# Linear attention with softmax features and a gated MLP: softmax without extrema, transposed queries, a lagging down projection

## The chip, the cores and the metric

One core of a Trainium2 chip runs the kernel. The metric is the device time of one execution in microseconds; the time before is 304.11 us, the median of three runs (303.58 to 304.22). The engines are PE (TensorE matmul, with its weight loads as PEld), DVE (VectorE), ACT (ScalarE), POOL (GpSimd) and SP, which issues most DMAs. Each works through its own instructions in order and waits on semaphores for the others.

## The reference

The input is 2048 tokens of width D = 512 in bf16; there are H = 32 heads of 16.

```python
mod = silu(c) @ w_mod                       # sa, ca, ga, sb, cb, gb
h = layernorm(x) * (1 + ca) + sa
q, k, v = split(h @ wqkv)                   # 32 heads of 16
pq, pk = q @ w_phi, k @ w_phi               # per head, 16 x 16
phi = concat(softmax(p), softmax(-p))       # 32 features, for q and for k
kv, z = phi_k^T v, sum_s phi_k              # per head
o = (phi_q kv) / (phi_q z + 1e-6)
x = x + ga * (o @ wo)
h = layernorm(x) * (1 + cb) + sb
x = x + gb * ((sigmoid(h @ w_gate) * (h @ w_up)) @ w_down)   # F = 1376
```

## The kernel before

Tokens are worked in 16 tiles of 128. The setup loads the weights through SP's queue, folds w_phi into the K part of wqkv (`fold_a_piece` transposes, `fold_b_piece` multiplies with the block diagonal `bd`, lines 226 to 248), computes the modulation columns `modc`, and normalizes the first tokens: `ln_stats` on DVE, `ln_small` and most `xn` on POOL, four transposes a column block on PE (`tp_h`), and the scaling into `h1T` on ACT or DVE.

The K loop (lines 476 to 522) runs over 20 items, the 16 K tiles and the first 4 Q tiles. An item is a software pipeline of stages: project into a PSUM bank (`p_bank`), take the largest and the smallest of each 16 on DVE (`s_maxmin`), subtract the largest from the bank by a matmul with the identity and exponentiate, undo it and subtract the smallest by two more matmuls and exponentiate the negative, sum and take reciprocals on DVE (`s`, `r`), multiply on POOL (`phi`). K tiles then add `phi` times `vaug` into `kvacc`; Q tiles are transposed by a DMA into `phiqT`.

When all K tiles are in, `kv_blockdiag` cuts out the head blocks, and the first four tiles pass through the attention output, the residual `x1` and the second LayerNorm one after the other (lines 515 to 529).

The GLU stretch goes over four chunks of 512 tokens. For each of 11 pieces of F it computes `g_ps` and `u_ps`, `tg` = tanh on ACT, `hm` on DVE, and at once four matmuls of the down projection into `y_ps`, which accumulate in four banks. Between the pieces, hooks work on the next chunk's queries, attention and LayerNorm. In the setup and the K loop the order on each engine is that of the program; in the GLU stretch a scheduler may interleave.

```python
            act.activation(tg[:fsz, :], g_ps[:fsz, :], ACT.Tanh, scale=0.5)
            dve.scalar_tensor_tensor(hm[:fsz, :], tg[:fsz, :], 1.0, u_ps[:fsz, :], op0=ALU.add, op1=ALU.mult)
            for tl in range(4):
                pe.matmul(y_ps[tl][:], lhsT=hm[:fsz, tl * P:(tl + 1) * P], rhs=wd_sb[:fsz, ft, :],
                          start=(ft == 0), stop=(ft == FT - 1))
```

In the profile nearly every instruction has line 47, that of the helper which records the order, so rows are told apart by the names of their tiles.

Of the kernel before, what the change touches and what calls it, by code (L numbers as in the profile page):

```python
# [9 lines left out]
BF16 = mybir.dt.bfloat16  # L10
ACT = mybir.ActivationFunctionType
ALU = mybir.AluOpType
AX = mybir.AxisListType

_SCHED = mybir.DependencyInfo(mybir.DependencyClass.NoSync, mybir.DependencyReason.SCHED_ONLY)


class _Ordered:

    def __init__(self, tc, eng):  # L20
        self._tc = tc
        self._eng = eng
        self._last = None
        self._fence = None
        self.strict = False

    def _note(self, r):
        ins = getattr(r, "ins", None)
        if ins is None:
            return r  # L30
        if self.strict and self._last is not None:
            self._tc.add_manual_dep(ins, self._last.name, _SCHED, reason="program order")
        elif self._fence is not None:
            self._tc.add_manual_dep(ins, self._fence.name, _SCHED, reason="phase fence")
        self._last = ins
        return r

    def fence(self):
        self._fence = self._last

    def __getattr__(self, name):
        f = getattr(self._eng, name)
        if not callable(f):
            return f

# [7 lines left out]
def kernel(  # L53
# [12 lines left out]
    CW = 68  # L66

    pe = _Ordered(tc, nc.tensor)
    act = _Ordered(tc, nc.scalar)
    dve = _Ordered(tc, nc.vector)  # L70
    pool = _Ordered(tc, nc.gpsimd)
    sp = _Ordered(tc, nc.sync)
    engines = (pe, act, dve, pool, sp)

    def set_strict(flag):
        for e in engines:
            if e.strict and not flag:
                e.fence()
            e.strict = flag

    consts = ctx.enter_context(tc.tile_pool(name="consts", bufs=1))
    psA_cm = tc.tile_pool(name="psA", bufs=1, space=bass.MemoryType.PSUM)
# [18 lines left out]
    ga_bc = consts.tile([P, D], FP32, name="ga_bc")
    gb_bc = consts.tile([P, D], FP32, name="gb_bc")
    mhalf = consts.tile([P, NT], FP32, name="mhalf")
    h1T = consts.tile([P, KT, S], BF16, name="h1T")
    vaug_all = consts.tile([P, NT, H, DH + 1], BF16, name="vaug_all")
    mask = consts.tile([P, 4, DH + 1], FP32, name="mask")
    kvbd_n = consts.tile([P, NG, 4 * DH], BF16, name="kvbd_n")
    kvbd_d = consts.tile([P, NG, 4], BF16, name="kvbd_d")
    stats = consts.tile([P, NT, 6], FP32, name="stats")
# [24 lines left out]
    sp.dma_start(x_sb[:, 0:4, :], x_v[:, 0:4, :])
    sp.dma_start(wqk_sb[:, :, D:2 * D], wqkv_v[:, :, D:2 * D])
# [13 lines left out]
    nc.gpsimd.memset(mhalf[:], -0.5)  # L149
    make_identity(nc, ident[:])  # L150
    bmask = setup.tile([P, P], BF16, name="bmask")
    make_block_diagonal(nc, bmask[:], DH)

    def ln_stats(src_ap, st, mvt, t):
        dve.bn_stats(st[:, t, :], src_ap)
        dve.bn_aggr(mvt[:, t, :], st[:, t, :])

    def ln_small(sl, mvt, vepst, rstdt, nmeant, nmrt=None):
        pool.tensor_scalar(vepst[:, sl], mvt[:, sl, 1], 1e-5, None, op0=ALU.add)
        pool.tensor_tensor(rstdt[:, sl], vepst[:, sl], mhalf[:, sl], op=ALU.pow)  # L160
        pool.tensor_scalar(nmeant[:, sl], mvt[:, sl, 0], -1.0, None, op0=ALU.mult)
        if nmrt is not None:
            pool.tensor_tensor(nmrt[:, sl], nmeant[:, sl], rstdt[:, sl], op=ALU.mult)

    def ln_xn(src_ap, t, rstdt, nmeant, nmrt, on_act):
        xn = lnp.tile([P, D], BF16, name="xn", tag="xn")
        if on_act:
            act.activation(xn[:], src_ap, ACT.Identity, scale=rstdt[:, t:t + 1], bias=nmrt[:, t:t + 1])
        else:
            pool.tensor_scalar(xn[:], src_ap, nmeant[:, t:t + 1], rstdt[:, t:t + 1], op0=ALU.add, op1=ALU.mult)  # L170
        return xn

    xn_box = {}

    def ln1_xn(t, on_act=False):
# [12 lines left out]
    def ln1_quarter(g, j, tag="tp"):
        ln_quarter([xn_box[4 * g + tl] for tl in range(4)], h1T[:, j, g * 512:(g + 1) * 512], j, 0, tag)

    ones11 = setup.tile([1, 1], BF16, name="ones11")
    nc.gpsimd.memset(ones11[:], 1.0)
    c_ps = ps_tile("c_ps", "tp", [P, 2 * KT])
# [15 lines left out]

# [434 lines left out]
```

## Time and profile before

| | |
|---|---|
| median of the runs | 304.11 us |
| profiled execution, span | 304.9 us |
| PE busy | 243.3 us (80%), 1524 matmuls seen |
| DVE busy | 193.2 us (63%) |
| ACT busy | 108.1 us (35%) |
| POOL busy | 116.0 us (38%) |
| mean granted clock of TensorE | 0.931 |

The busy shares are averages over stages that differ, so the rows below are cut by stage: setup to 17.5 us, K loop to 93.5, first attention tiles to 126 (the first `g_ps` starts at 125.9), GLU to 298.6. A granted clock of 1.00 is 2.4 GHz, 0.50 is 1.2 GHz. Matmul durations overlap, since the engine is pipelined; their pace is read from the starts.

### The profile page before, as it was taken

Reading aid. Unit: us, or ns where it says so; the run is one execution under the profiler, and the core shown is the slowest. Engines: PE = TensorE matmul, PEld = TensorE weight load, DVE = VectorE, ACT = ScalarE, POOL = GpSimd, SP = SyncE. Lnnn points to the kernel's source line nnn. Section 1 sums busy time; section 2 is a strip of 40 time slices with the busy share of each in tenths; the row PEclk is TensorE's granted clock in tenths of the full one; section 3 lists DMA queues with packets and bytes.
Section 4 is the critical chain, followed back from the end, with each engine's and each line's share of the span. In section 5 each row is a group of like instructions: output and inputs, shape, how many; then the busy total and the mean of one; then the engine's idle time right before and its main releaser. Section 6 shows DMA issues by size and latency. Waiting matters only on the chain. (4 is left out here: it accounts for less than half of the span.)

```text
span 304.9 us, 4096 instructions
## 1 busy us (share of the span) xinstructions
PE 243.3 (80%) x1524; PEld 115.6 (38%) x1552; DVE 193.2 (63%) x334; ACT 108.1 (35%) x185; POOL 116.0 (38%) x126
## 2 busy tenths in 40 slices
PE   0566988889774574599997899988799989499991
PEld 0533444444331342244443444443344443243330
DVE  3288899677989552167886288677287778052223
ACT  2454776765334033324311433301433311422110
POOL 2847379652556543974502222501313311400000
PEclk9995999999869567599999999999999999999996
DMA  6999400000001410001450021450021340020002
GB/s 186 384 399 400 153 2 1 1 2 0 2 0 34 85 21 0 0 0 35 71 105 0 0 69 37 70 105 1 0 69 38 69 91 14 0 69 0 2 0 69
DMA packets 31989, 19.71 MB, mean 65 GB/s; under 512 B 23921, under 2 KB 29410, under 8 KB 31970
## 3 DMA queue, kind: packets, MB, share of 16 engines
q1 hardware_dynamic: 31938, 19.44, 23.0%
q8 instruction: 12, 0.20, 0.3%
q0 software_dynamic: 32, 0.02, 0.2%
q14 instruction: 7, 0.06, 0.1%
HBM read 11.58 MB, written 2.10 MB: 45 GB/s over the span
## 5 line engine op out<-in xcount | busy, mean ns | idle before, releaser
L47 POOL TENSOR_TENSOR phi<-e,r 128x1024 bf16<-128x1024 bf16 x32 | 61.6, 1928 | 80.5 <-DVE r L47 65.2
L47 ACT ACTIVATE tg<-g_ps 128x512 bf16<-128x512 f32 (+1 forms) x44 | 26.2, 596 | 85.1 <-PE g_ps L47 76.5
L47 ACT ACTIVATE e<-p_bank 128x512 bf16<-128x512 f32 x64 | 38.3, 598 | 45.5 <-PE p_bank L47 43.1
L47 DVE SCALAR_TENSOR_TENSOR hm<-tg,u_ps 128x512 bf16<-128x512 bf16 (+1 forms) x44 | 30.0, 682 | 38.2 <-PE u_ps L47 28.4
L47 PE MATMUL g_ps<-h2T,wg_sb 128*128 128x512 bf16 (+1 forms) x170 | 49.2, 384 | 4.2 <-ACT tg L47 2.2
L47 PE MATMUL y_ps<-wd_sb,hm 128*128 128x512 bf16 (+1 forms) x170 | 46.3, 381 | 1.1 <-DVE hm L47 0.8
L47 PE MATMUL u_ps<-h2T,wu_sb 128*128 128x512 bf16 (+1 forms) x171 | 46.4, 385 | 0.5
L47 DVE TENSOR_REDUCE s<-e 128x64 f32<-128x1024 bf16 x32 | 38.6, 1207 | 6.5 <-ACT e L47 6.5
L47 PE MATMUL p_bank<-wqk_f,h1T 128*128 128x512 bf16 x125 | 35.3, 394 | 1.5 <-ACT h2T L47 1.3
L47 DVE TENSOR_REDUCE nmx<-p_bank 128x32 bf16<-128x512 f32 x32 | 21.5, 672 | 20.3 <-PE p_bank L47 20.3
L47 PEld LDWEIGHTS <-h1T 128*128 128x128 bf16 x192 | 19.2, 101 | 26.1 <-issue 6.5
L47 POOL TENSOR_SCALAR veps<-mv 128x4 f32<-128x4 f32 (+1 forms) x11 | 2.5, 228 | 62.7 <-DVE mv L47 57.2
L47 PEld LDWEIGHTS <-wg_sb 128*128 128x128 bf16 (+1 forms) x176 | 17.3, 101 | 22.3 <-issue 5.2
L47 PEld LDWEIGHTS <-hm 128*128 128x128 bf16 (+1 forms) x176 | 14.3, 97 | 27.8 <-DVE hm L47 16.9
L47 PEld LDWEIGHTS <-wu_sb 128*128 128x128 bf16 (+1 forms) x176 | 17.5, 101 | 19.1 <-issue 1.1
L47 DVE TENSOR_REDUCE nmn<-p_bank 128x32 bf16<-128x512 f32 x32 | 21.5, 672 | 0.0
L47 PE MATMUL tp_h<-ident,xn 128*128 128x128 bf16 x112 | 12.1, 239 | 11.7 <-POOL xn L47 10.7
L47 PE MATMUL a_ps<-wo_sb,oT 128*128 128x512 bf16 x62 | 18.6, 423 | 3.2 <-ACT oT L47 2.9
L47 PE MATMUL p_bank<-nmx,nident 128*128 128x512 bf16 x32 | 12.5, 391 | 8.6 <-ACT e L47 8.5
L47 DVE RECIPROCAL r<-s 128x64 f32<-128x64 f32 x32 | 17.6, 550 | 2.2
L47 PEld LDWEIGHTS <-xn 128*128 128x128 bf16 x128 | 9.5, 109 | 23.4 <-POOL xn L47 14.8
L47 PE MATMUL v_ps<-wv_sb,h1T 128*128 128x512 bf16 x58 | 17.0, 397 | 0.7 <-ACT h1T L47 0.4
(83 smaller groups left out, 286.8 us busy)
## 6 DMA issues: line engine op xcount, KB each, us to landing
x_sb<-in_A_x_dram SPq DMA_DIRECT2D x4, 512.0 KB, 10.0
wmod_sb<-in_w_mod_dram SPq DMA_DIRECT2D x1, 2048.0 KB, 14.8
out_dram<-ot SPq DMA_DIRECT2D x16, 128.0 KB, 1.8
wg_sb<-in_B_w_gate_dram SPq DMA_DIRECT2D x1, 1376.0 KB, 17.8
wu_sb<-in_B_w_up_dram SPq DMA_DIRECT2D x1, 1376.0 KB, 18.1
wd_sb<-in_B_w_down_dram SPq DMA_DIRECT2D x1, 1280.0 KB, 16.7
wqk_sb<-in_A_wqkv_dram SPq DMA_DIRECT2D x2, 512.0 KB, 8.2
wmod_sb<-in_w_mod_dram SPq DMA_DIRECT2D x1, 1024.0 KB, 8.3
```

The lines of the kernel that those rows point to most:

```text
L47: return self._note(f(*a, **k))
```

## The change

The kernel is written anew with every engine's order by hand:

- Softmaxes take no extrema: exp(p) and exp(-p) come straight from the projection. A bound on |p| is computed on the chip from the folded weights and the modulation; a flag says whether it is too large, and after the last output a branch runs a general path with extrema and writes all outputs again.
- K tiles keep sum, reciprocal and `phi`; LayerNorm's `xn` moves from POOL to DVE. `kvacc` holds 8 heads by 136 columns instead of 4 by 68.
- Queries are projected transposed (`q_blk`: weights as the stationary side, 512 tokens as the moving one), exponentiated into `eT` with no sums and no transposes. Sums and denominators come out of small matmuls (`sm`), four small DVE ops form the factors `cc`, and each of the two halves of the numerator is multiplied by its factor (`u`); the Q weights for the fold are transposed by their load.
- The chunks are of 2, 2, 4, 4, 4 tiles, and the down projection of a chunk is issued during the next one, tile by tile in two banks; the last chunk's follows at the end. The attention and LayerNorm steps of later tiles are put between the pieces by a list of due times.

On DVE, in the K loop, a tile before (`nmx`, `nmn` extrema, `s` and `r` sum and reciprocal):

```order
L47 BN_STATS stats<-x_sb 128x6
L47 BN_AGGR mv<-stats 128x2
L47 TENSOR_REDUCE nmx<-p_bank 128x32
L47 TENSOR_REDUCE nmn<-p_bank 128x32
L47 TENSOR_REDUCE s<-e 128x64
L47 RECIPROCAL r<-s 128x64
```

The same place now, tile 3 and the beginning of tile 4 (`ksum` and `kr` are sum and reciprocal):

```order
L130 BN_STATS st_77<-x_sb 128x6
L131 BN_AGGR mv_78<-st_77 128x2
L235 TENSOR_REDUCE ksum<-e 128x64
L237 RECIPROCAL kr<-ksum 128x64
L141 TENSOR_SCALAR xn<-x_sb,mv_78,rs_80 128x512 x4
```

The extrema are gone, and four `xn` stand behind the sum of a group's last tile.

On ACT, in the K loop, before:

```order
L47 CAST vaug_all_81<-v_ps_406 128x32x16
L47 ACTIVATE h1T_80<-tp_h_426,modc_76 128x512
L47 ACTIVATE e_434<-p_bank_392 128x32x16 x2
L47 CAST vaug_all_81<-v_ps_441 128x32x16
L47 ACTIVATE h1T_80<-tp_h_469,modc_76 128x512
L47 COPY wT0_477<-tp_w_478 128x512
```

and now (`e` and `h1T` as before; the bank `tp_h` of a tile is the next token group's):

```order
L226 CAST vaug1_108<-v_ps_329 128x32x16
L152 ACTIVATE h1T_70<-tp_h_340,modc_75 128x512
L231 ACTIVATE e_346<-k_ps_335 128x512 x2
L226 CAST vaug2_109<-v_ps_357 128x32x16
L152 ACTIVATE h1T_70<-tp_h_368,modc_75 128x512
```

`e` of a tile stands behind the `h1T` written in that tile, as it did before; what feeds that `h1T` is now the `xn` above, and POOL's `phi` and `rstd` ahead of it.

On PE, in a chunk of four tiles of the GLU stretch, before (`y_ps0` to `y_ps3` are the four tiles of the same chunk):

```order
L47 LDWEIGHTS wg_sb_71
L47 MATMUL g_ps_2882<-h2T_2765,wg_sb_71 128x512
L47 LDWEIGHTS hm_2876
L47 MATMUL y_ps0_2824<-wd_sb_73,hm_2876 128x512
L47 LDWEIGHTS hm_2876
L47 MATMUL y_ps1_2825<-wd_sb_73,hm_2876 128x512
L47 LDWEIGHTS hm_2876
L47 MATMUL y_ps2_2826<-wd_sb_73,hm_2876 128x512
L47 LDWEIGHTS hm_2876
L47 MATMUL y_ps3_2827<-wd_sb_73,hm_2876 128x512
L47 LDWEIGHTS wu_sb_72
L47 MATMUL u_ps_2883<-h2T_2765,wu_sb_72 128x512
```

and now (chunk 2; `hm_1605` belongs to chunk 1):

```order
L602 LDWEIGHTS wu_sb_68
L602 MATMUL u_ps_2023<-h2T_1675,wu_sb_68 128x512
L570 LDWEIGHTS hm_1605
L570 MATMUL y_ps_1973<-wd_sb_69,hm_1605 128x512
L570 LDWEIGHTS hm_1605
L570 MATMUL y_ps_1973<-wd_sb_69,hm_1605 128x512
L597 LDWEIGHTS wg_sb_67
L597 MATMUL g_ps_2033<-h2T_1675,wg_sb_67 128x512
```

The `hm` that a weight load takes was written a chunk earlier, and consecutive `y_ps` matmuls go to one tile.

The diff replaces nearly every line; its core, with the functions that are new:

```diff
-        dve.tensor_reduce(nmx[it][:], bv, axis=AX.X, op=ALU.max, negate=True)
-        dve.tensor_reduce(nmn[it][:], bv, axis=AX.X, op=ALU.min, negate=True)
...
-        act.activation(e_t[it][:, :, 0, :], bv, ACT.Exp)
+    def k_exp(t):
+        e_t[t] = ph1.tile([P, 2, H, DH], BF16, name="e", tag="e", bufs=3)
+        for s in range(2):
+            act.activation(e_t[t][:, s].rearrange("p h j -> p (h j)"), k_ps[t][:], ACT.Exp, scale=1.0 - 2.0 * s)
+    def ln1_xn(t):
+        dve.tensor_scalar(xn[:], x_sb[:, t, :], mv1[:, t, 0:1], rs1[:, t:t + 1], op0=ALU.subtract, op1=ALU.mult)
+    def q_blk(cq, blk, b):
+        ps = bank(b, "q_ps")
+        for j in range(KT):
+            pe.matmul(ps[:], lhsT=wqk_f[:, j, blk * P:(blk + 1) * P], rhs=h1T[:, j, cq * 512:(cq + 1) * 512],
+                      start=(j == 0), stop=(j == KT - 1))
+        for s in range(2):
+            act.activation(eT[:, s * 4 + blk, cq * 512:(cq + 1) * 512], ps[:], ACT.Exp, scale=1.0 - 2.0 * s)
...
+    for i in range(NT):
+        g, j = i // 4 + 1, i % 4
+        k_v(i)
+        k_vaug(i)
+        if j == 0 and g < 4:
+            for t in range(4 * g, 4 * g + 4):
+                ln1_xn(t)
+        k_k(i)
+        if g < 4:
+            ln1_quarter(g, j, 7, on_dve=False)
...
+        k_exp(i)
+        if i >= 3:
+            k_kv(i - 3, kvacc, vaug[(i - 3) % VS])
+        if i >= 1 and g < 3:
+            ln_stats(x_sb[:, 4 * g + 4 + j, :], st1, mv1, 4 * g + 4 + j)
+            if j == 3:
+                ln_rstd(slice(4 * g + 4, 4 * g + 8), mv1, ve1, rs1)
...
+        k_norm(i)
...
+        def a_num(p, q, via_pe):
...
+                u = ph2.tile([P, H, DH], BF16 if via_pe else FP32, name=f"u{s}", tag=f"u{s}", bufs=2)
+                dve.tensor_tensor(u[:], ps[:].rearrange("p (h d) -> p h d", d=DH),
+                                  c_t[p][:, q, s, :].unsqueeze(2).to_broadcast([P, H, DH]), op=ALU.mult)
...
+            at(b, lambda p=p: a_sm(p), 0.5)
...
+                while did < per and npend:
+                    f = next(pending, None)
...
+    with tc.If(fv_box[0] > 0, preferred_fallthrough_block=False):
...
```

## Rows read from the trace of the kernel before

**Rows 1.** busy by stage: start:end, us; PE, PEld, DVE, ACT, POOL; clock, DMA, GB/s

```profile
0.00:17.50 17.50, 6.31 (x85) 5.83 (x86) 6.04 (x15) 6.29 (x13) 10.26 (x26) 1.00 0.89 301
17.50:93.50 76.00, 62.12 (x441) 31.28 (x448) 65.13 (x106) 43.80 (x77) 43.15 (x37) 0.91 0.23 84
93.50:126.00 32.50, 15.69 (x121) 8.32 (x122) 16.34 (x35) 10.05 (x16) 17.18 (x24) 0.69 0.18 33
126.00:298.60 172.60, 159.15 (x883) 70.18 (x899) 103.70 (x177) 47.92 (x80) 45.42 (x41) 0.99 0.18 37
```

**Rows 2.** list of waits: who waited for whom, us, times, longest

```profile
PEld L47 <- DVE hm L47: 16.9, 40, 1.3
```

**Rows 3.** chain of waits: start, us, what, in the last chunk

```profile
290.36 0.86 PE u_ps L47 x4
```

**Rows 4.** timeline of one tile of the K loop: start, us, instruction

```profile
40.00 1.21 DVE L47 TENSOR_REDUCE s<-e 128x64 f32<-128x1024 bf16 x1
40.47 0.42 PE L47 MATMUL kvacc<-vaug_all,phi 128*128 128x68 bf16 x8
40.72 0.38 PE L47 MATMUL tp_h<-ident,xn 128*128 128x128 bf16 x4
41.24 0.55 DVE L47 RECIPROCAL r<-s 128x64 f32<-128x64 f32 x1
41.71 0.64 DVE L47 BATCH_NORM_STATS2 stats<-x_sb 128x6 f32<-128x512 bf16 x1
42.48 0.66 DVE L47 TENSOR_REDUCE nmx<-p_bank 128x32 bf16<-128x512 f32 x1
```

**Rows 5.** timeline of the setup, POOL and DVE

```profile
12.64 1.14 POOL L47 TENSOR_TENSOR bd<-wp_sb,bmask 128x512 bf16<-128x512 bf16 x1
18.16 0.68 DVE L47 BATCH_NORM_STATS2 stats<-x_sb 128x6 f32<-128x512 bf16 x1
21.93 1.04 POOL L47 TENSOR_TENSOR rstd<-veps,mhalf 128x4 f32<-128x4 f32 x1
```

**Rows 6.** instructions by form: busy us, mean ns of one, idle before

```profile
L47 ACT ACTIVATE e<-p_bank 128x512 bf16<-128x512 f32 x64 | 38.3, 598 | 45.5 <-PE p_bank L47 43.1 <-POOL phi L47 2.0
L47 POOL TENSOR_TENSOR phi<-e,r 128x1024 bf16<-128x1024 bf16 x32 | 61.6, 1928 | 80.5 <-DVE r L47 65.2 <-issue 8.8 <-ACT h1T L47 3.5
L47 DVE TENSOR_TENSOR x<-a_ps,x_sb 128x512 f32<-128x512 f32 x12 | 8.3, 690 | 1.3 <-PE a_ps L47 0.8
L47 ACT ACTIVATE h1T<-tp_h,modc 128x512 bf16<-128x512 bf16 x12 | 9.3, 778 | 4.9 <-PE tp_h L47 4.9
L47 DVE TENSOR_SCALAR h1T<-tp_h,modc 128x512 bf16<-128x512 bf16 x4 | 2.1, 536 | 1.4 <-PE tp_h L47 1.4
L47 DVE SCALAR_TENSOR_TENSOR hm<-tg,u_ps 128x512 bf16<-128x512 bf16 x40 | 27.3, 682 | 28.5 <-PE u_ps L47 26.3 <-PE p_bank L47 2.1
L47 POOL TENSOR_TENSOR wd_sb<-wd_sb,gb_bc 128x512 bf16<-128x512 bf16 x11 | 12.3, 1161 | 0.0
L47 DVE TENSOR_TENSOR kvbd_n<-kvacc,mask 128x256 bf16<-128x256 f32 x2 | 0.8, 389 | 0.0
L47 DVE TENSOR_TENSOR kvbd_d<-kvacc,mask 128x16 bf16<-128x16 f32 x2 | 0.3, 164 | 0.0
```

**Rows 7.** busy time in two pieces of the K loop's beginning

```profile
22.00:24.00 2.00, 0.00 (x0) 0.00 (x0) 1.97 (x6) 0.41 (x1) 1.85 (x4) 0.93 1.04 375
28.00:30.00 2.00, 2.00 (x6) 0.75 (x5) 1.97 (x5) 0.56 (x1) 1.90 (x4) 0.50 1.02 395
```

**Rows 8.** timeline of the tail, DVE

```profile
300.60 1.29 DVE L47 TENSOR_TENSOR ot<-y_ps,x 128x512 bf16<-128x512 f32 x2 [1.31 <-DMA out_dram<-ot]
```

**Rows 9.** DMA issues: size of each, us from issue to landing

```profile
wmod_sb<-in_w_mod_dram SPq DMA_DIRECT2D x1, 2048.0 KB, 14.8
out_dram<-ot SPq DMA_DIRECT2D x16, 128.0 KB, 1.8
phiqT<-phi SPq DMA_TRANSPOSE x16, 3.1
```

More of the change, by code (lines that the diff above doesn't have):

```diff
@@ L65 @@
     NG = 8
[L66 to L82, printed above, removed]
@@ L101 @@
[L101 to L109, printed above, removed]
@@ L147 @@
     sp.dma_start(wd_sb[0:F_LAST, FT - 1, :], B_w_down[(FT - 1) * P:F, :])
-    nc.gpsimd.memset(mhalf[:], -0.5)
+    pool.memset(ones11[:], 1.0)
     make_identity(nc, ident[:])
[L151 to L163, printed above, removed]
@@ L188, in ln1_quarter @@
[L188 to L193, printed above, removed]
+    pool.memset(bmask[:], 1.0)
+    pool.affine_select(out=bmask[:], in_=bmask[:], compare_op=ALU.is_ge, fill=0.0, base=0,
+                       pattern=[[-DH, 8], [0, DH]], channel_multiplier=1)
+    pool.affine_select(out=bmask[:], in_=bmask[:], compare_op=ALU.is_ge, fill=0.0, base=DH - 1,
+                       pattern=[[DH, 8], [0, DH]], channel_multiplier=-1)
@@ new lines, with ln1_quarter @@
+    xn_box = {}
+    def ln1_xn(t):
+        xn = ph1.tile([P, D], BF16, name="xn", tag="xn", bufs=8)
+        dve.tensor_scalar(xn[:], x_sb[:, t, :], mv1[:, t, 0:1], rs1[:, t:t + 1], op0=ALU.subtract, op1=ALU.mult)
+        xn_box[t] = xn
+    def ln1_quarter(g, j, b, on_dve):
+        tp = bank(b, "tp_h", [P, 512], BF16)
+        for tl in range(4):
+            pe.transpose(tp[:, tl * P:(tl + 1) * P], xn_box[4 * g + tl][:, j * P:(j + 1) * P], ident[:])
+        dst = h1T[:, j, g * 512:(g + 1) * 512]
+        if on_dve:
+            dve.tensor_scalar(dst, tp[:], modc[:, 4 + j:5 + j], modc[:, j:j + 1], op0=ALU.mult, op1=ALU.add)
+        else:
+            act.activation(dst, tp[:], ACT.Identity, scale=modc[:, 4 + j:5 + j], bias=modc[:, j:j + 1])
@@ L194 @@
+    c_ps = bank(7, "c_ps", [P, 2 * KT])
     for j in range(KT):
@@ L327, in s_proj_a @@
-    def s_proj_a(it):
-        kind, t = it
-        if kind == 'K':
-            s_proj_v(t)
-    def s_proj_b(it):
-        kind, t = it
-        tok = slice(t * P, (t + 1) * P)
-        bank[it] = ps_tile("p_bank", ps_state["bank_tag"])
-        if kind == 'K':
-            for j in range(KT):
-                pe.matmul(bank[it][:], lhsT=h1T[:, j, tok], rhs=wqk_f[:, j, D:2 * D], start=(j == 0), stop=(j == KT - 1))
-        else:
-            for j in range(KT):
-                pe.matmul(bank[it][:], lhsT=h1T[:, j, tok], rhs=wqk_f[:, j, 0:D], start=(j == 0), stop=(j == KT - 1))
@@ L430, in att_out @@
-    def att_out(t, tag, x1_via_act):
-        a_ps = ps_tile("a_ps", tag)
-        for j in range(KT):
-            pe.matmul(a_ps[:], lhsT=oT[t][:, j, :], rhs=wo_sb[:, j, :], start=(j == 0), stop=(j == KT - 1 and not x1_via_act))
-        x1[t] = rot_ref[0].tile([P, D], FP32, name="x1", tag="x1", bufs=8)
-        if x1_via_act:
-            pe.matmul(a_ps[:], lhsT=ident[:], rhs=x_sb[:, t, :], start=False, stop=True)
-            act.copy(x1[t][:], a_ps[:])
-            ln_stats(a_ps[:], stats2, mv2, t)
-        else:
-            dve.tensor_tensor(x1[t][:], a_ps[:], x_sb[:, t, :], op=ALU.add)
-            ln_stats(x1[t][:], stats2, mv2, t)
@@ new lines, with k_v @@
+    pool.memset(ones_f[:], 1.0)
+    pool.tensor_copy(kvbd[:, :, P + 8:P + 16],
+                     bmask[:].rearrange("p (h f) -> p h f", f=DH)[:, :, 0].unsqueeze(1).to_broadcast([P, NG, 8]))
+    kvacc = [bank(i, f"kvacc{i}", [P, 512]) for i in range(3)]
+    e_t, phi_t, v_ps, k_ps = {}, {}, {}, {}
+    def k_v(t):
+        v_ps[t] = bank(3 + t % 2, "v_ps")
+        for j in range(KT):
+            pe.matmul(v_ps[t][:], lhsT=h1T[:, j, t * P:(t + 1) * P], rhs=wv_sb[:, j, :], start=(j == 0), stop=(j == KT - 1))
@@ new lines, in k_k, with k_vaug @@
+    def k_k(t):
+        k_ps[t] = bank(5 + t % 2, "k_ps")
+        for j in range(KT):
+            pe.matmul(k_ps[t][:], lhsT=h1T[:, j, t * P:(t + 1) * P], rhs=wqk_f[:, j, D:2 * D], start=(j == 0), stop=(j == KT - 1))
+    def k_vaug(t):
+        act.copy(vaug[t % VS][:, :, 0:DH], v_ps.pop(t)[:].rearrange("p (h d) -> p h d", d=DH))
+    def k_exp(t):
+        e_t[t] = ph1.tile([P, 2, H, DH], BF16, name="e", tag="e", bufs=3)
+        for s in range(2):
+            act.activation(e_t[t][:, s].rearrange("p h j -> p (h j)"), k_ps[t][:], ACT.Exp, scale=1.0 - 2.0 * s)
@@ new lines, in k_norm, with k_kv @@
+    def k_norm(t):
+        sm = ph1.tile([P, 2, H], FP32, name="ksum", tag="ksum", bufs=2)
+        dve.tensor_reduce(sm[:], e_t[t][:], axis=AX.X, op=ALU.add)
+        r = ph1.tile([P, 2, H], FP32, name="kr", tag="kr", bufs=3)
+        dve.reciprocal(r[:], sm[:])
+        phi_t[t] = ph1.tile([P, 2, H, DH], BF16, name="phi", tag="phi", bufs=3)
+        pool.tensor_tensor(phi_t[t][:], e_t[t][:], r[:].unsqueeze(3).to_broadcast([P, 2, H, DH]), op=ALU.mult)
+    def k_kv(t, kvacc, va):
+        ph = phi_t.pop(t)
+        for g in range(NG):
+            s, blk = g // 4, g % 4
+            pe.matmul(kvacc[g // 3][:, (g % 3) * 136:(g % 3) * 136 + 136],
+                      lhsT=ph[:, s, blk * 8:(blk + 1) * 8, :].rearrange("p h j -> p (h j)"),
+                      rhs=va[:, blk * 8:(blk + 1) * 8, :].rearrange("p h d -> p (h d)"),
+                      start=(t == 0 and g % 3 == 0), stop=(t == NT - 1), skip_group_check=True)
@@ new lines, in bound_c, with load_flag @@
+    def bound_c():
+        ps = bank(4, "bnd", [1, 3])
+        pe.matmul(ps[:], lhsT=ones_f[:], rhs=bst[:], start=True, stop=True)
+        dve.tensor_copy(bs[0:1, 0:3], ps[:])
+        dve.tensor_tensor(bs[0:1, 3:4], bs[0:1, 1:2], bs[0:1, 2:3], op=ALU.mult)
+        dve.scalar_tensor_tensor(bs[0:1, 4:5], bs[0:1, 0:1], float(D), bs[0:1, 3:4], op0=ALU.mult, op1=ALU.add)
+        dve.tensor_scalar(flag[:], bs[0:1, 4:5], BOUND2 / 2.0, 0.0, op0=ALU.is_le, op1=ALU.is_equal)
+    def load_flag():
+        fv_box.append(nc.values_load(flag[0:1, 0:1], min_val=0, max_val=1,
+                                     skip_runtime_bounds_check_because="written as 0 or 1"))
```

845 lines of the change are left out of this document (435 added, 410 removed).

## The prediction, made before the result was known

> **What bounds the kernel now.** I read the busy table by stage first [rows 1]. The reader is to see four stages of different kind: a setup of 17.5 us, a K loop of 76 us in which VectorE is the fullest engine (65.1 of 76.0) and TensorE waits for it, a stretch of 32.5 us (93.5 to 126) in which no engine is half full except POOL and the granted clock is 0.69, and the GLU stretch, where TensorE is busy 159.2 of 172.6 at 0.99. So the first 126 us are a matter of VectorE and of latency, the rest one of TensorE and of its waits. Of those the list of waits names the down projection: 40 waits of a weight load for hm, 16.9 us [rows 2]. The price of a matmul of 512 columns is 0.215 us, four in 0.86 [rows 3].
>
> Inside the K loop one tile shows its cost [rows 4]: the sum over e and its reciprocal take from 40.00 to 41.71, 1.71 us; the LayerNorm statistics that follow take until 42.48, 0.77 us; then come the two extrema, of which the first shown takes 0.66.
>
> **What the change does to each engine.** By the instruction lists TensorE goes from 1,552 matmuls with 500.8 thousand columns to 1,493 with 461.9 thousand on the path that runs (the rest stands behind the branch): 96 correction matmuls go (20.6 us), the doubled width of kv and num comes back (some 7 us). At 0.215 us for 512 columns that is 194 us of pure TensorE. VectorE loses 64 extrema, 16 query sums and reciprocals, and gains 16 more multiplications u (two a tile) and the small ops on the denominators. The total does not decide; I go through it stage by stage.
>
> *To the first exponentials.* bd stood behind two xn on POOL and ended at 13.78 [rows 5]; now POOL computes it first, and the fold can start when the four K transposes are copied, about 3.4 us earlier; but all four fold copies are now on ScalarE, 1.1 us more. So the statistics of the second token group, at 18.16 before [rows 5], start at 15.9. Four of them at 0.8 are done at 19.1; rstd on POOL (its piece of 1.04 [rows 5] and a small add) at 20.5. Then four xn, new on VectorE. No row shows VectorE on this operand; the nearest is h1T at 0.536 [rows 6], POOL paid more; between nothing and 0.69 I take 0.54: 22.6. Transposes 0.4, h1T on ScalarE 0.78, two exp 0.6 each [rows 6]: first e at 25.
>
> The Trainium skill (VectorE: DVE Perf Modes, The perf-mode tier table) lets tensor_scalar run four bf16 elements a cycle from SBUF, which would make xn an estimated 0.2; the same skill (SBUF — State Buffer, Who interferes with whom) says such an op, and one with two SBUF inputs, must wait while POOL reads SBUF. No row here shows either. By the first the four xn cost 0.8 instead of 2.2; by the second they would wait out one phi and cost about 2.7.
>
> *The K loop.* With the extrema gone, a tile costs VectorE 1.71 + 0.77 = 2.5, with hops 2.6, as long as statistics of later tokens lie between (8 tiles), and TensorE 8 x 0.215 + 0.22 for four transposes + twice the 0.25 of the narrower kv [rows 4] = 2.4 (7 steps). POOL's phi, 1.93 [rows 6], hides under both, and so do ScalarE's two e, vaug (priced as an e) and h1T, 2.6 by durations that overlap a little at their ends. 8 x 2.6 + 7 x 2.4 = 37.6; the folds of Q and gb add 1.7 of TensorE.
>
> The new order has a weak place at each token group (tiles 4 and 8). On ScalarE h1T of the next group now stands ahead of exp, in front of it the transposes on TensorE, and these need xn, which is behind the sum of tile 3 on VectorE and behind rstd on POOL, itself behind phi of tile 2. From the end of exp(3): sum and reciprocal 1.8; phi(2) and rstd end at 2.6; four xn to 4.8; transposes and h1T to 5.9; ScalarE had 0.6 to do and goes on with exp only then. A group boundary costs 4.6, twice 9.2. While it lasts TensorE is idle, and what idling does the clock rows show [rows 7]: nothing ran from 22 to 24, and at 28 to 30 the clock stood at 0.50, the lower level of 1.2 GHz. A tile needs TensorE for 4.8 at that level; I take 2.3 lost after each of the two boundaries and 1.0 in the first group, together 5.6. exp(15) ends at 25 + 37.6 + 1.7 + 9.2 + 5.6 = 79.1.
>
> *Hand-over.* sum and reciprocal 1.8, phi 1.9, kv 0.6, block diagonal (three pieces of at most 0.55 by 0.389 for 256 elements and three small ones of 0.16 [rows 6]) 2.1: 85.5. The query exponentials, 4.8 of ScalarE, hide there.
> Then a chain up to the first gate matmul: matmuls and copy of sm 1.3, four small VectorE ops 1.3, two u 1.4, the second num 0.5, two u 1.4 (5.9); tpo and its copy behind two exp 1.6 (7.5); a_out 1.1, x1 0.7, the second a_out, waiting for the same bank, 1.7, x1 and statistics 1.5 (12.5); small ops 1.3, two u 1.4, two xn 1.4, two u 1.4 (18.0); transposes 0.6, h2T 0.9, oT copy 0.6, a_out 1.0, a query block 0.9: 22.0. Before it stood 32.5 us in this place [rows 1]. For the clock in it I add 1.5: first gate matmul at 109, against 126 before.
>
> *The two chunks of two tiles.* By the list TensorE has 18.8 and 19.2 us of columns there; VectorE 11 hm of half width (0.39 by the row for 256 elements), 8 u, 3 or 4 x1 at 0.69 with statistics, two sets of small ops, h2T: 19 and 23. They alternate through two banks for num and one for a_out and the query blocks, so I take 45 for both, between 38 (TensorE alone) and 58.
> *The other three chunks.* 29.2 + 68.7 of TensorE by the list. The down projection multiplies the chunk before, whose hm is long written: the 16.9 us of [rows 2] have nothing left to wait for. 97.9 + 1 = 99, so the last matmul ends at 253.
> *Tail.* ot 0.7; from the end of the last ot (300.60 + 0.68, in a pair of 1.29 [rows 8]) the span took 3.0 more. The flag is loaded and branched on by every engine; TensorE and ScalarE do so early, VectorE and SP at the end. No row prices a taken branch: between nothing and 6, I take the 1.8 of one output store [rows 9]. Tail 5.5: 258.5.
>
> Costed at nothing: the transposing load of the Q weights (512 KB; phiqT, half of it, landed in 3.1 [rows 9]) delays the loads behind it by some 6 us at most, but the first of these, the rest of wmod, 14.8 to landing [rows 9], is used after tile 3, past 30 us. If it took 25 us instead, tile 3 would hold TensorE by about 15. The scaling of wd on POOL (1.16 each [rows 6], 11 of them) has the whole first chunk to hide in.
>
> The sum is against the profiled execution's 304.9, which lies 0.8 above the median of 304.1: 258.5 becomes 258.
>
> **Rivals.**
> A, quicker: the group boundaries overlap better than I add them up and the small chunks run at TensorE's pace: 9.2 + 5.6 of the K loop and 5 of 45 go: 240. For it speaks that start to start VectorE's ops lie closer than their durations; against it that the xn chain has no second path.
> B, VectorE held by POOL: the small ops, which have two SBUF inputs, and xn wait for POOL's wd_scale, o and phi. Four sets of three ops, each behind one 1.16, are 14 us in the chunks where VectorE is already the fullest: 272. The Trainium skill's page on SBUF (Who interferes with whom) states this as an exclusive lock; before, no VectorE op beside phi had two SBUF inputs or a fast mode, so the trace is silent.
> C, slower than before: the clock stays at 1.2 GHz from the end of the K loop through both small chunks. 14 us of TensorE work in the chain and 38 in the chunks would double: +52, 310. It decides where more than 46 us of matmul run at the low level. For it: 0.69 in the stretch from 93.5 to 126 at 48% busy. Against it: 0.99 over the GLU stretch at 92% busy [rows 1], and the small chunks are denser than the former.
> D, the change doesn't do what it says: the bound fails and the general path runs. Entries of the folded weight have a spread of 4 x 0.05 x 0.0125 = 0.0025 by the reference's scales, row maxima near 0.0085; 512 x 512 x 0.0085 squared is 19 against the limit of 392. If it ran: 32 tiles of some 5.6 us of VectorE in series, 180, and everything after the K loop again, some 150: near 590.
>
> **How the numbers follow.** Forecast 0.56 (its own range 248 to 268), A 0.22, B 0.18, C 0.03, D 0.01. The time is the forecast's. The range runs from A's 240 to a little over B's 272, 276. A difference of 0.2% (0.6 us) is the least that this measurement tells from none. Forecast, A and B are faster: 0.96; of C 0.01 lies within 0.2%, 0.02 above; with D slower 0.03.
>
> **What would show it.** Right: sum over e every 2.6 us inside a group of four, with gaps of VectorE's sums of about 7 at tiles 4 and 8; first gate matmul near 109; no weight load waiting for hm; TensorE over 95% busy in the last 70 us. Wrong: gaps above 10 in the K loop or a half-rate clock past 115 (C); m, cc or xn on VectorE several times as long as their sizes (B); a POOL or TensorE instruction of the general path after the last store (D).

## The result, and the profile after

The changed kernel took 281.13 us (278.11 to 282.04) beside 304.05 for the kernel before: ratio 0.920, 95% interval 0.913 to 0.927. The forecast was 258, the range 240 to 276. The sign was right; half of the forecast gain is missing. Four executions of the runs below (one of e3, one of e4, two of e8) fell in a slower state of the chip and are left out of their medians.

The busy table of the changed kernel, cut where the forecast's terms end (columns as in [rows 1]; one cut, at 139.50, lies just before the second small chunk, whose first gate matmul starts at 140.33):

```profile
0.00:21.83 21.83, 11.02 (x99) 7.63 (x100) 11.96 (x30) 9.12 (x17) 7.89 (x25) 0.93 0.93 301
21.83:79.11 57.28, 46.15 (x324) 25.48 (x323) 37.20 (x52) 35.23 (x66) 29.38 (x18) 0.85 0.24 89
79.11:87.85 8.74, 5.66 (x47) 3.19 (x46) 5.84 (x13) 4.35 (x9) 4.37 (x3) 1.00 0.00 1
87.85:110.77 22.92, 16.24 (x139) 9.11 (x138) 14.42 (x30) 10.40 (x20) 3.31 (x4) 0.93 0.01 1
110.77:139.50 28.73, 22.23 (x194) 15.62 (x193) 20.65 (x40) 11.87 (x27) 16.50 (x17) 0.94 0.08 19
139.50:167.60 28.10, 21.70 (x190) 14.94 (x190) 21.33 (x51) 8.63 (x20) 7.64 (x9) 1.00 0.14 34
167.60:225.00 57.40, 50.89 (x281) 23.82 (x281) 36.87 (x77) 16.39 (x27) 7.95 (x11) 1.00 0.18 44
225.00:274.20 49.20, 49.17 (x229) 22.33 (x227) 22.22 (x40) 8.95 (x15) 0.00 (x0) 1.00 0.07 25
274.20:279.70 5.50, 0.00 (x0) 0.00 (x0) 0.69 (x1) 0.00 (x0) 0.00 (x0) 0.85 0.11 33
```

| term | forecast | measured |
|---|---|---|
| first e exponential at | 25 | 21.8 |
| from there to the end of exp(15) | 54.1 | 57.3 |
| hand-over to the block diagonal | 6.4 | 8.7 |
| chain to the first gate matmul | 23.5 | 22.9 |
| two small chunks | 45 | 56.9 |
| three big chunks | 99 | 106.6 |
| tail | 5.5 | 5.5 |
| sum | 258.5 | 279.7 |

The first gate matmul came at 110.8, forecast 109. Of the 21 us by which the span exceeds the sum, 19.5 lie behind that matmul: 11.9 in the small chunks, 7.6 in the big ones. In the small chunks TensorE was busy 77%, from 167.6 to 225 it was 89%, and from 225 on it never stopped.

Three places of this trace show what the waits looked like. The first is a boundary in the K loop, VectorE and then POOL (start, duration):

```profile
34.47 3.07 DVE L141 TENSOR_SCALAR xn<-x_sb,mv,rs 128x512 bf16<-128x512 bf16 x4
```
```profile
34.49 1.93 POOL L239 TENSOR_TENSOR phi<-e,kr 128x1024 bf16<-128x1024 bf16 x1
```

Four xn took 3.07 here, but 1.73 at the start, where no phi ran. The second is in the first small chunk: VectorE, POOL and TensorE (in brackets the idle time before and who ended it):

```profile
116.16 2.03 DVE L445 TENSOR_SCALAR xn<-x,mv,rs 128x512 bf16<-128x512 f32 x2
118.11 1.25 DVE L384 TENSOR_TENSOR m<-smS 128x128 f32<-128x128 f32 x1
```
```profile
115.44 3.77 POOL L330 TENSOR_TENSOR wd_sb<-wd_sb,gbx 128x512 bf16<-128x512 bf16 x3
```
```profile
118.25 0.40 PE L460 MATMUL tp_x<-ident,xn 128*128 128x128 bf16 x4 [0.90 <-DVE xn L445]
121.23 1.01 PE L400 MATMUL num<-kvbd,eT 128*128 128x128 bf16 x8 [2.59 <-DVE h2T L464]
```

m takes 0.26 to 0.29 elsewhere; beside the scaling of wd it took 1.25. TensorE's num waits for a bank that h2T, behind all of this on VectorE, has yet to empty. The third is early in the fourth chunk: VectorE, POOL, ScalarE and TensorE:

```profile
203.70 1.22 DVE L440 SCALAR_TENSOR_TENSOR nmr<-mv,rs 128x2 f32<-128x2 f32 x1 [0.58 <-POOL rs L135]
```
```profile
203.64 1.26 POOL L409 TENSOR_TENSOR o<-u,u 128x512 bf16<-128x512 f32 x1
```
```profile
204.95 0.81 ACT L447 ACTIVATE xn<-x,nmr,rs 128x512 bf16<-128x512 f32 x1 [5.63 <-DVE nmr L440]
205.67 0.58 ACT L599 ACTIVATE tg<-g_ps 128x512 bf16<-128x512 f32 x1
```
```profile
206.30 1.02 PE L597 MATMUL g_ps<-h2T,wg_sb 128*128 128x512 bf16 x4 [1.94 <-ACT tg L599]
```

A tanh stands in the queue behind an xn that waits 5.6 us for nmr, and TensorE waits for the tanh. The nmr itself, a product of 128x2, took 1.22 beside POOL's sum o and ended with it; without one it takes 0.15. So POOL holds VectorE here too, and not by the scaling of wd.

TensorE's idle time in the small chunks can be named wait by wait. In the first, 6.5 us: 2.6 for the query exponentials to leave a bank that a_ps shares, 2.6 for h2T in the lines above, 1.3 for xn. In the second, 6.4 us: 4.1 for hm, 1.8 for a tanh, 0.4 for a transpose. The longest wait for hm, VectorE and TensorE:

```profile
162.11 1.27 DVE L402 TENSOR_TENSOR u<-num,cc 128x512 f32<-128x512 f32 x2
163.30 0.41 DVE L603 SCALAR_TENSOR_TENSOR hm<-tg,u_ps 128x256 bf16<-128x256 bf16 x1
```
```profile
163.76 0.60 PE L602 MATMUL u_ps<-h2T,wu_sb 128*128 128x256 bf16 x4 [1.72 <-DVE hm L603]
```

The hm stands behind two u, and the next u_ps needs the bank that hm reads: the kernel gives gate and up two banks each in its first chunk, and one each from the second on.

### The profile page after: what moved, and what is told of

Same layout as the page of the kernel before. It is cut to its first block, busy times and chain, and to the rows that moved or that the text cites. A ratio compares the mean times of both kernels' runs of the same rounds, so it can differ in the third digit from the quotient of the medians.

```text
span 279.7 us, 3972 instructions
## 1 busy us (share of the span) xinstructions
PE 223.1 (80%) x1494; PEld 122.1 (44%) x1494; DVE 171.2 (61%) x330; ACT 104.9 (38%) x197; POOL 77.0 (28%) x85
## 4 chain that ended last, share of the span: by engine, by line
PE 54%; DVE 18%; issue 7%; POOL 6%; ACT 6%; DMA 5%; SPq 2%; POOLq 0%; DVEq 0%; ACTq 0%
PE y_ps L570 10%; PE g_ps L597 9%; PE u_ps L602 9%; PE v_ps L218 5%; PE k_ps L223 4%; PE a_ps L428 4%; PE q_ps L253 4%; PE kvacc L245 3%; DVE st L130 3%; DMA wp_sb<-in_A_w_phi_dram 2%; PE tp_h L147 2%; POOL phi L239 2%; DVE u L402 2%; POOL rs L135 2%; DVE xn L141 2%
## 5 line engine op out<-in xcount | busy, mean ns | idle before, releaser
L603 DVE SCALAR_TENSOR_TENSOR hm<-tg,u_ps 128x512 bf16<-128x512 bf16 (+3 forms) x55 | 31.7, 577 | 46.2 <-PE u_ps L602 33.2
L599 ACT ACTIVATE tg<-g_ps 128x512 bf16<-128x512 f32 (+3 forms) x55 | 28.0, 509 | 70.7 <-PE g_ps L597 68.3
L597 PE MATMUL g_ps<-h2T,wg_sb 128*128 128x512 bf16 (+3 forms) x220 | 47.5, 339 | 5.0 <-ACT tg L599 4.9
L602 PE MATMUL u_ps<-h2T,wu_sb 128*128 128x512 bf16 (+3 forms) x220 | 47.1, 337 | 4.3 <-DVE hm L603 4.1
L239 POOL TENSOR_TENSOR phi<-e,kr 128x1024 bf16<-128x1024 bf16 x16 | 30.8, 1927 | 29.9 <-DVE kr L237 21.8
L235 DVE TENSOR_REDUCE ksum<-e 128x64 f32<-128x1024 bf16 x16 | 19.3, 1208 | 18.0 <-ACT e L231 18.0
L256 ACT ACTIVATE eT<-q_ps 128x512 bf16<-128x512 f32 x32 | 17.4, 595 | 16.9 <-PE q_ps L253 16.9
L402 DVE TENSOR_TENSOR u<-num,cc 128x512 f32<-128x512 f32 (+1 forms) x32 | 20.4, 681 | 0.8 <-PE num L400 0.6
L152 ACT ACTIVATE h1T<-tp_h,modc 128x512 bf16<-128x512 bf16 x14 | 10.9, 779 | 21.8 <-PE tp_h L147 21.7
L223 PE MATMUL k_ps<-wqk_f,h1T 128*128 128x512 bf16 x64 | 19.0, 426 | 0.0
L253 PE MATMUL q_ps<-h1T,wqk_f 128*128 128x512 bf16 x64 | 18.2, 410 | 0.0
## 6 DMA issues: line engine op xcount, KB each, us to landing
wg_sb<-in_B_w_gate_dram SPq DMA_DIRECT2D x1, 1376.0 KB, 12.5
```

The source lines that it names most:

```text
L223: pe.matmul(k_ps[t][:], lhsT=h1T[:, j, t * P:(t + 1) * P], rhs=wqk_f[:, j, D:2 * D], start=(j == 0), stop=(j == KT - 1))
L235: dve.tensor_reduce(sm[:], e_t[t][:], axis=AX.X, op=ALU.add)
L239: pool.tensor_tensor(phi_t[t][:], e_t[t][:], r[:].unsqueeze(3).to_broadcast([P, 2, H, DH]), op=ALU.mult)
L253: pe.matmul(ps[:], lhsT=wqk_f[:, j, blk * P:(blk + 1) * P], rhs=h1T[:, j, cq * 512:(cq + 1) * 512], start=(j == 0), stop=(j == KT - 1))
L402: dve.tensor_tensor(u[:], ps[:].rearrange("p (h d) -> p h d", d=DH), c_t[p][:, q, s, :].unsqueeze(2).to_broadcast([P, H, DH]), op=ALU.mult)
L597: pe.matmul(g_ps[:fsz, 0:n], lhsT=wg_sb[:, j, ft * P:ft * P + fsz], rhs=h2T[k][:, j, 0:n], start=(j == 0), stop=(j == KT - 1))
```

## The experiments

Ratios are to the kernel before on the same chip, where its median was 305.6 to 306.6. Unedited stretches differ by some 2.5 us from profile to profile (the block diagonal starts at 84.3 to 86.8 where the K loop is unedited), so stages are compared beside totals. For the totals of e1 and e2 this matters: their intervals overlap that of the changed kernel (0.913 to 0.927), and what they show is shown by the stages. The table has starts in us in the profiled executions: first exponential of K, block diagonal, first gate matmul, the chunk behind the first four tiles (the third, with chunks of four the second), last output; then the median.

```
run          first e  kvbd   first g  after 4 tiles  last ot   median
changed        21.8   86.2    110.8      167.6        274.2    281.1
e1_qbank       21.6   84.4    107.6      162.8        269.4    277.5
e2_nowd        21.6   86.0    108.4      163.5        270.1    277.2
e3_xnpool      21.6   84.3    107.5      166.4        279.8    287.3
e8_xnadd       21.8   84.5    107.7      163.0        273.1    280.1
e6_nolag       21.7   84.7    107.9      173.5        279.3    285.6
e7_four        21.8   86.8    117.0      154.2        267.8    274.3
e4_kq          15.9   88.8    113.3      170.3        276.8    281.1
e5_kq2         16.5   73.7     98.2      156.3        262.8    268.0
e9_best        16.5   72.5    102.7      138.4        252.5    260.5
e10_late       15.5   73.2    105.3      147.1        259.8    265.2
e11_wddve      16.7   76.2    104.5      136.8        250.7    257.4
```

**The shared bank.**

```diff
-at(6.0 + 3.0 * k, lambda f=f: f(7), 0.9)
+at(6.0 + 3.0 * k, lambda f=f: f(4), 0.9)
```

> The query blocks that are spread over the two small chunks go to bank 4 instead of bank 7, which they share with the output projection a_ps. In the changed kernel TensorE waited there 4 times, 2.9 us, for the exponentials to leave the bank. Theory 1 (the small chunks lose their time to in-order queues and shared banks, many small waits): the 4 waits go, first gate matmul of the third chunk 2 to 4 us earlier, 278 to 279 us against 281.1. Theory 2 (VectorE held by POOL is what the chunks wait for): the wait only moves to the next VectorE result, within 1 us of 281.

Ratio 0.910 (0.903 to 0.917). The waits for the exponentials went; the first chunk is 2.4 shorter (27.2; 29.6 to 29.7 in the changed kernel, e3, e4 and e8), the second 0.8 longer. The bank is worth 1.6; the rest of the 3.6 in the medians lies ahead of the edit.

**POOL's scaling of wd left out** (`wd_scale(ft)` deleted).

> Leaves out the scaling of the down weights by the gate on POOL (11 multiplications of 1.16 us; so the output lacks that factor). Theory 2 (rival B of the prediction, VectorE held by POOL): m at 118.11 (1.25 us), den at 127.97 (1.20), the two xn at 116.16 (2.03) go back to 0.28, 0.23 and 1.57, and the two small chunks, 57 us now, shorten by 5 or more: 276 or less. Theory 1: these three rows shorten by about 2.4 together, of which at most 2 reach the end: 279 to 281.

Ratio 0.906 (0.900 to 0.912). VectorE, the same place:

```profile
113.81 1.00 DVE L445 TENSOR_SCALAR xn<-x,mv,rs 128x512 bf16<-128x512 f32 x2
114.73 0.28 DVE L384 TENSOR_TENSOR m<-smS 128x128 f32<-128x128 f32 x1
```

Two xn take 1.00 instead of 2.03, m 0.28 instead of 1.25: POOL does hold VectorE. But den, expected back at 0.23, still takes 1.20, beside POOL's o. The price of the scaling is 1.8 in the first chunk, nothing in the second, and 0.8 to 2.1 in the chain before (22.4 from block diagonal to first gate matmul; 23.2 to 24.6 without the edit). The total, 277.2, fits neither theory, 276 or less and 279 to 281. Rival B's mechanism is real, its 14 us are not: the five kinds of small VectorE operations behind the block diagonal (m, den, cc, nmr, xn) took together about 5.8 longer beside POOL's work in the changed kernel than they take alone.

**xn on POOL**, in two forms.

```diff
-act.activation(xn, x1, ACT.Identity, scale=rs2, bias=nmr2)
+pool.tensor_scalar(xn, x1, mean, rs2, op0=ALU.subtract, op1=ALU.mult)   # e3
+pool.tensor_scalar(xn, x1, -mean, rs2, op0=ALU.add, op1=ALU.mult)       # e8
```

> The second LayerNorm's xn of token pairs 2 to 7 goes from ScalarE to POOL (0.77 us each there in the kernel before), without the small nmr on VectorE. In the changed kernel ScalarE's tanh stood in its queue behind an xn that waited for nmr, 19.3 us in all; TensorE waited for a tanh 4.9 us in 5 places. Theory 1: those 5 waits go, and xn comes one hop earlier, 3 to 5 us: 276 to 278. Theory 2: 12 more POOL operations hold VectorE more often, 281 or above.

> As run e3_xnpool, xn of token pairs 2 to 7 on POOL, but as (x + (-mean)) * rstd, the form of the kernel before (0.77 us there), since (x - mean) * rstd took POOL 2.07 us. If the form alone makes the difference: xn takes 0.77 again, no tanh stands behind an xn, chunk 3 (34.0 us in the changed kernel, 38.9 in e3_xnpool) takes 31 to 32, chunk 4 32: 277 to 279. If the extra operations on POOL, or its hold on VectorE, make it: above 281.

e3: ratio 0.948 (0.940 to 0.956), slower than the changed kernel. e8: 279.92 and 280.18, no gain clear of noise; from the first gate matmul to the last output it takes 165.4 against 163.4. POOL in e3, then in e8, SP's queue in e8 and TensorE in e8:

```profile
181.58 4.14 POOL L447 TENSOR_SCALAR xn<-x,mv,rs 128x512 bf16<-128x512 f32 x2
```
```profile
164.86 1.52 POOL L447 TENSOR_SCALAR xn<-x,nmr,rs 128x512 bf16<-128x512 f32 x2
```
```profile
165.65 1.19 SPq L472 DMA_TRANSPOSE xnT<-xn  x1
166.89 1.26 SPq L422 DMA_TRANSPOSE oT<-o  x1
```
```profile
169.58 0.81 PE L428 MATMUL a_ps<-wo_sb,oT 128*128 128x512 bf16 x3 [2.06 <-DMA oT<-o]
```

The form explains the 2.07 against 0.76. But with the cheap form, which frees ScalarE, the third chunk still takes 38.0 instead of 34.0 and the fourth 33.7 instead of 34.1. TensorE no longer waits for a tanh, but 9.0 us for oT in the whole run instead of 2.1. The transpose of oT stands behind that of xn in SP's queue, 1.2 us each; it does so in the changed kernel too, where it is issued 1.0 behind the chunk's first gate matmul and here 3.9. What made it later was not isolated (POOL now has nmr and xn behind o). My theory that the tanh's place in the queue costs 3 to 5 us fell: the wait went and another took its place.

**The K loop.** The next group's xn earlier, transposed in halves, exp ahead of h1T; in the second form xn between the sum and the reciprocal:

```diff
 dve.tensor_reduce(sm[:], e_t[t][:], axis=AX.X, op=ALU.add)
+for tx in xns:            # e5; in e4 behind the reciprocal
+    ln1_xn(tx)
 dve.reciprocal(r[:], sm[:])
```

> In the K loop the next token group is prepared earlier: statistics one tile earlier, rstd on POOL ahead of the third phi of a group, two of the four xn before the group's boundary, transposes in halves in the second and third tile, with exp ahead of h1T on ScalarE. If the two boundaries cost what the prediction said, 4.6 each plus about 4 of half clock behind them, the gaps between the sums over e of 7.3 and 7.9 us at tiles 4 and 8 fall to about 3.5, and the last exponential of K comes 8 to 12 us earlier: 270 to 273. If VectorE's own work sets the loop (2.5 a tile and the xn), only 3 us come back: 278.

> The K loop of run e4_kq again, with xn on VectorE moved between the sum over e and its reciprocal, where the phi of the tile before has ended and the next has not begun, and with the folds of Q back in their old order. In e4_kq every xn that met a phi took as long as that phi: two xn 2.33 us beside a phi of 1.93, 0.43 each without one. Theory P (POOL's phi holds VectorE's xn, and that cost the gain): xn take 0.43 each, the gaps between the sums over e at the group boundaries are 3 to 4 us instead of 7.3 and 7.9, the block diagonal of kv starts at 74 to 79 instead of 86: 270 to 275. Theory L (the loop is bound by the latency from exp over sum, phi and kv): block diagonal at 82 to 86, 278 to 282.

e4: ratio 0.918 (0.911 to 0.925), no gain; the block diagonal starts at 88.8, later than in any other run. e5: 0.873 (0.866 to 0.880). VectorE and POOL in e4:

```profile
33.19 2.33 DVE L141 TENSOR_SCALAR xn<-x_sb,mv,rs 128x512 bf16<-128x512 bf16 x2
```
```profile
33.44 1.93 POOL L249 TENSOR_TENSOR phi<-e,kr 128x1024 bf16<-128x1024 bf16 x1 [0.96 <-DVE kr L247]
```

and in e5:

```profile
29.76 0.72 DVE L141 TENSOR_SCALAR xn<-x_sb,mv,rs 128x512 bf16<-128x512 bf16 x2
30.40 0.54 DVE L249 RECIPROCAL kr<-ksum 128x64 f32<-128x64 f32 x1
```
```profile
31.11 1.93 POOL L251 TENSOR_TENSOR phi<-e,kr 128x1024 bf16<-128x1024 bf16 x1 [1.42 <-DVE kr L249]
```

An xn that meets a phi ends with it (35.5 after 35.4); placed in the hole between two phi it takes 0.36 here and 0.39 in the next pair. (Later the hole is missed in part: two xn take 0.92 and 1.57.) In e5 the gaps of the sums at the boundaries fell from 7.3 and 7.9 to 3.0 and 2.4. The first e comes 5.3 earlier since exp no longer stands behind h1T, and from there to exp(15) it takes 50.1 instead of 57.3, so the block diagonal starts 12.5 earlier than in the changed kernel. Theory L, at 82 or later, is out, and the signs of theory P came. Yet e4 had also put the folds of Q behind exp, which e5 took back (TensorE waits 1.3 for them instead of 3.0), and e5 has the earlier preparation of e4 besides; how the other 7.2 divide among these edits no run shows.

**The parts undone.** No lag (`for f in down_mms(k)` behind each chunk), and `CHUNKS = [4, 4, 4, 4]` with the second pair finished before the loop.

> Undoes one part of the change: the down projection of a chunk follows its own chunk at once, instead of being spread over the next. If the prediction's step holds (the lag removes the waits for hm), TensorE or its weight loads wait for hm again at the end of each chunk, and the gate and up matmuls of a chunk have nothing between them but the events: TensorE waits for tanh and hm in every step of chunks 2 to 4. I expect 10 to 17 us more than the changed kernel: 291 to 298. If the lag is worth nothing, 281.

> Undoes another part: four chunks of four tiles instead of 2, 2, 4, 4, 4; the second token pair is then finished ahead of the first gate matmul. First gate matmul 10 to 13 us later (121 to 124 instead of 111), but the first four tiles then need one pass of the gate and up weights less (2 us of half-empty steps) and every small operation hides under steps twice as long. If the small chunks lose 12 us by their shortness (waits between short steps): the end comes within 2 us of the changed kernel, or before it. If they lose it to the work that has to lie in front of chunk 2 anyway, the end is 8 to 12 us later: 289 to 293.

e6: ratio 0.930 (0.926 to 0.935), 4.5 over the changed kernel in the medians and 8 from first gate matmul to last output: less than expected. And no weight load waits for hm here either: with the down projection behind its whole chunk hm is written in time, so that wait of [rows 2] went with the move out of the single step, not with the lag. Nor does TensorE wait more for tanh and hm, as expected without the lag: 5.4 in all behind the first gate matmul, against 9.0. Of the 8 us it idles 2.3 and is busy 5.7. The longest wait, in the middle of a down projection:

```profile
209.15 1.89 PE L428 MATMUL a_ps<-wo_sb,oT 128*128 128x512 bf16 x4 [3.58 <-DMA oT<-o]
```

From 208 to 215 the granted clock was 0.51, the lower level; the same four matmuls take 1.03 at the upper one. What the lag by itself is worth stays open.

e7: ratio 0.895 (0.891 to 0.899), 7 us better. The first gate matmul is 6.2 later, and from there to the last output it is 150.8 instead of 163.4. The busy table of e7 from the first gate matmul on, by chunk:

```profile
117.00:154.20 37.20, 30.86 (x193) 15.11 (x195) 26.53 (x49) 13.81 (x25) 17.18 (x17) 0.93 0.13 29
154.20:192.60 38.40, 35.06 (x209) 17.36 (x214) 25.48 (x55) 9.74 (x16) 6.91 (x8) 1.00 0.17 38
192.60:229.30 36.70, 34.69 (x198) 16.80 (x199) 25.93 (x53) 10.11 (x17) 6.87 (x8) 1.00 0.18 44
229.30:267.80 38.50, 38.33 (x176) 17.27 (x177) 18.43 (x35) 6.56 (x11) 0.00 (x0) 1.00 0.08 29
```

TensorE idles 12 us in 151, against 19.4 in 163.4. The first four tiles take 37.2 in one chunk and 56.9 in two; but the two chunks also hold work that e7 has elsewhere (37.8 us of columns against 26.3, the down projection of the first two tiles for one), so it is the 6.8 of the medians that counts. The run undoes more than the width of the steps: all four first tiles now have two banks each for gate and up, and the due times moved.

**Together.** e9 is e5, e7 and e1; e10 is e9 with xn three places later and the pairs' start earlier; e11 is e9 with the scaling of wd on VectorE in tiles 10 to 15 (and the gate's row `gb_mm` six tiles earlier):

```diff
+if t >= 10:
+    for ft in range(2 * (t - 10), min(2 * (t - 10) + 2, FT)):
+        dve.tensor_tensor(wd_sb[:, ft, :], wd_sb[:, ft, :], gb_bc[:], op=ALU.mult)
```

> Puts together what helped alone: the K loop of e5_kq2, four chunks of four tiles (e7_four) and the query blocks in bank 4 (e1_qbank). If the gains lie in different stages and add up (13.1 for the K loop, 6.8 for the chunks, 2 to 3 for the bank, which with chunks of four is waited for 2.3 us instead of 2.9): 259 to 261. If the K loop's gain is lost again because the first chunk then meets loads or POOL's scaling of the weights: 265 or above.

> As e9_best, with the second LayerNorm's xn 3 places of the schedule later behind its rstd, and the pairs' start 2 to 8 places earlier, so that ScalarE's tanh stands less often behind an xn that waits. In e7_four TensorE waited 2.2 us for a tanh, once. If that wait is what the queue order costs: 2 us less than e9_best. If it turns into a wait for the transposes on SP's queue, as in e8_xnadd: as e9_best or up to 3 us more.

> As e9_best, with the down weights scaled on VectorE, two in each of the tiles 10 to 15 of the K loop between the sum over e and its reciprocal, instead of on POOL beside the first chunk. VectorE is busy 12.2 of 21.8 us there. If POOL's scaling held VectorE in the chain and in the first chunk (e2_nowd without it: 3.9 us less): block diagonal 0 to 2 us later, first gate matmul at most 1 later, first chunk 1.5 to 2.5 shorter, in all 1 to 3 us less than e9_best. If the twelve more operations push back kv: 2 us more.

e9: 0.853 (0.847 to 0.858), 260.5 us; the gains add up as expected (259 to 261). e10: 0.868 (0.864 to 0.873), slower than e9: the wait for the tanh fell to 0.7, but the first chunk takes 41.8 instead of 35.8. TensorE waits 3.5 there for u on VectorE (0.2 in e9), at a granted clock of 0.86 instead of 0.89. e11: 0.842 (0.836 to 0.847), the quickest of all, 257.4 us; block diagonal 3.7 later (expected 0 to 2), first gate matmul 1.8 later (at most 1), first chunk 3.5 shorter (32.3), of which TensorE is busy 2.0 less, at a granted clock of 0.95 instead of 0.89.

## Why the prediction was wrong

*What failed: "They alternate through two banks ..., so I take 45 for both, between 38 (TensorE alone) and 58."* It came out at 56.9, almost the upper bound: 5.9 more of work than the 38, and 5.9 more of waits than the 7 allowed on top.

TensorE was busy 43.9. The narrow matmuls for the sums sm are one reason:

```profile
114.27 0.55 PE L376 MATMUL sm<-kvbd,eT 128*128 128x16 bf16 x16
114.68 0.60 PE L597 MATMUL g_ps<-h2T,wg_sb 128*128 128x256 bf16 x4
```

From start to start the 16 matmuls of 16 columns take 0.41, where their columns say 0.11; four such sets make 1.2. From 121.0 to 124.5 the granted clock was at the lower level (0.51 from 121 to 124), which costs an estimated 1.6. The other 3 are not taken apart; part of them is that busy times count each group to its end (four gate matmuls 0.60) and the columns only its pace (0.43).

The waits were 12.9, each named above. The bank shared with the query blocks is shown by e1 (2.6 of wait, 1.6 net) and POOL's hold on VectorE ahead of h2T and xn by e2 (1.8). The waits for hm and tanh in the second chunk, 5.9, are seen in the trace and not isolated. One account is that a half-width step of 0.87 is too short to hide the 0.7 to 1.3 of VectorE work that stands in front of hm; another is that gate and up have one bank each from that chunk on. The trace has no wait for hm in the first chunk (half width, two banks each) and none in the big ones (full width, one each), as if it took both. No run separates them: e7, which gains 6.4 up to the last output although its first gate matmul is 6.2 later, changes both at once.

*The second failed term: "97.9 + 1 = 99"* for the big chunks, 106.6. TensorE was busy 2.2 more than its columns, and idle 6.5 instead of 1, all ahead of 225: 3.1 behind a tanh, 1.7 for oT, 1.0 for u, 0.4 for x1. That the tanh's place in the queue is the cause was tried three ways (e3, e8, e10), and each time the time came back as another wait. What would fill these chunks stays open.

*Right:* the gate and up matmuls and the down projection without a weight load waiting for hm, the tail with the branch (5.5), TensorE dense over the last 49 us, the boundaries of the K loop (7.2 between sums; 7.3 and 7.9) and the half clock behind them: the first sums of a group come 1.2, 2.1 and 1.9 later than 2.6, where the forecast had 1.0 and twice 2.3 (the granted clock was 0.50 from 40 to 42 and from 57 to 59). One cause in the boundaries was not in the forecast's chain but in its aside: POOL's phi held the four xn, 3.07 and 2.98 instead of 2.2, where the aside gave 2.7.

*Right by luck:* the first gate matmul, within 1.8. The first e was 3.2 early and the K loop 3.2 long. The hand-over was 2.3 longer: the last kv matmuls start 1.2 behind their phi, after other work of TensorE, and the scaling of wo holds the block diagonal, at 86.22, another 1.1:

```profile
83.82 2.48 DVE L310 TENSOR_TENSOR wo_sb<-wo_sb,ga_ps 128x512 bf16<-128x512 bf16 x4 [2.79 <-PE ga_ps L263]
```

The transposing load of the Q weights, costed at nothing with some 6 us of delay, held its queue for 9.96, and nothing waited for the loads behind it.

*The rivals:* A did not come, though e5 shows that the boundaries could be had back (its own terms, 9.2 + 5.6 + 5, give 239 and not 240). B holds in kind, in the K loop, the chain and the chunks. The Trainium skill (SBUF — State Buffer, Who interferes with whom) gives the rule of an exclusive lock, and the trace agrees: two xn took 2.33 beside a phi of 1.93, 0.72 without. By the same skill (VectorE: DVE Perf Modes, The perf-mode tier table) an xn was an estimated 0.2; the runs show 0.34 to 0.43 without a phi. C did not come: the granted clock is 0.93 or more in every stage from the block diagonal to the last matmul.

The range was too narrow because only the small chunks had an upper bound. With their 58 the sum is 271.5, still inside; with the big chunks' 106.6 as well it is 279.

## What to carry to other kernels

Price a stage of many short steps by the busy share that TensorE shows in stages with like waits (77% in the small chunks, 81% in the K loop), not by its columns plus a few us; here the columns left out both the waits and the cost of narrow matmuls. Before cutting steps to half their width, list what stands ahead in each in-order queue and how many banks let TensorE run ahead. A VectorE operation that meets a GpSimd one as xn met phi is priced by the GpSimd one; in e5 it was better placed where that engine waits for VectorE anyway. Before moving an operation out of one queue, look for the next queue on its way: here three such moves gave a new wait each.

## What the runs showed of the hardware

On POOL (x - mean) * rstd took 2.07 us and (x + (-mean)) * rstd 0.76, same shapes and types. The transposing load from DRAM of 512 KB held SP's queue from 4.78 for 9.96 us; an SBUF transpose of 128x512 held it 1.2. A product of 128x2 on VectorE took 0.15 us alone and 1.22 beside a GpSimd sum of 1.26. Sixteen matmuls of 16 columns took 0.41 us.
